# Masks of the second batch by matrix products, its maxima and differences from PSUM, one exponential per pair of heads

## Chip, cores and metric

One Trainium2 chip, one core of it. The metric is the device time in microseconds (us) of one launch; less is better. "PE" is TensorE, "DVE" VectorE, "ACT" ScalarE, "POOL" GpSimd, "SP" the queue that issues the DMAs.

## What is computed

Eight batches of windowed attention feed a two-layer feed-forward net. Cut to what matters:

```python
# q, k, v: (8, 8, 576, 64); heads 0..3 plain window of 32, heads 4..7 window 128, every 4th position
scores = 1/sqrt(64) * q @ k.T
scores = where(mask[head], scores, -1e9)
scores = scores - max(scores, axis=-1)
attn = exp(scores); attn = attn / (sum(attn, axis=-1) + 1e-9)
x = (attn @ v) as (4608, 512)
h = x @ w_in                       # (512, 2048)
out = where(h > 0, h, exp(min(h, 0)) - 1) @ w_out
```

## The kernel before

**Stages.** Attention of batch 0 runs first (`first_attention`, lines 338 to 386). Then the feed-forward net runs over the tokens: three passes of 512 tokens (`c` = 0, 1, 2), each with 16 steps `f` over the 2048 hidden columns, and after them a second form over larger blocks with fewer products. The attention of a later batch is woven into the pass before the tokens are needed; that of batch 1 (`second_attention`, lines 904 to 933) lies in pass `c` = 0, one or two pieces per step `f`.

**Batch 1.** It has four pairs of heads. A pair has two banks of scores in PSUM (`a_ps0`, `a_ps1`, one per head, 96 partitions by 6 x 64) and three pieces of work. E (lines 913 to 921): 72 small products for the scores, then on DVE masks added from PSUM into the SBUF tile `sm` (line 397), maxima over groups of 64 (line 410) and a scaling of the maxima (line 413), then on ACT six exponentials of 96x64, each with its own bias and with its sum accumulated (line 389). X (lines 422 to 436): six more such exponentials, the reciprocal of the sums on DVE (lines 326, 327), the product with them on POOL (line 328), 32x32 transposes on DVE (line 432), and copies into the operand `pt`, three on ACT and three on POOL (line 435). O (lines 924 to 932): products with `v` into the same two banks, then copies to `x32` on ACT (lines 314, 317). The pieces come in the order E0 X0 E1 X1 O0, a gap, E2 X2 O1, a gap, E3 X3, a gap, O2 O3. `sm` has a single buffer, so pair 1 may write it only when the copies of pair 0 have read it, and O0 may write the banks only when E1 has been read out of them.

**Beside it in pass 0.** The weights come as 64-bit floats. ACT scales the upper words (line 136), DVE puts 32-bit floats together in three steps (lines 144, 152, 154), and each is split into a high part on ACT and a low part on DVE (lines 191, 193). Step `f` computes a bank `h` (12 products of 512 columns, 8 with high weights and then 4 with low ones), ACT and DVE apply the activation (lines 627, 629, 632 or 634), and `o_ps` collects the second layer.

**Order.** PE works in program order: every product goes through `mm` (line 111). The other engines' order is made when the program is built, by a scheduler with an estimate of each instruction's duration, within `issue_after` bounds: the conversion of a weight block waits behind `maxima[-1]`, the splitting of x behind `masked[-1]`. So one changed piece moves neighbours on DVE, ACT and SP, up to the start of the second form, whose order is written out.

Of the kernel before, what the change touches and what calls it, by code (L numbers as in the profile page):

```python
# [15 lines left out]
AF = mybir.ActivationFunctionType  # L16
ALU = mybir.AluOpType
# [7 lines left out]
G = 32  # L25
QB = 3 * G
NU = S // QB
# [47 lines left out]
def body(ctx: ExitStack, tc: tile.TileContext, q, k, v, masks, w_in, w_out, out):  # L75
# [34 lines left out]
    def mm(*args, **kw):  # L110
        return inorder(nc.tensor.matmul(*args, **kw))  # L111
# [182 lines left out]
    def scores(s_ps, qt, kt, start):  # L294

        for n in range(NU):
            for c in range(GU):
                for h in range(2):
                    score(s_ps[h][:, n * 2 * G:(n + 1) * 2 * G], qt, kt, h, n, c, start, start or n == NU - 1)
# [85 lines left out]
        a_ps = ps_f.tile([P, 2, TC], F32, name="db"[hp % 2])  # L385
        yield outputs(0, hp, [(a_ps[:, i, :], i * NA, (i + 1) * NA) for i in range(NU // NA)], vt, tr, inorder)

    def exponential(u, sm, nmx, sums):
        nc.scalar.activation(out=sm[:, u, :], in_=sm[:, u, :], func=AF.Exp, bias=nmx[:, u:u + 1], scale=0.125, accum_out=sums[:, u:u + 1])  # L389

    def masks_added(hp, places, sm, eng=nc.vector):

        dil = hp >= NPAIR // 2
        for i in range(max(len(p) for p in places)):
            for h in range(2):
                n0, n1, s_ps = places[h][i]
                last = eng.tensor_tensor(out=sm[:, h * NU + n0:h * NU + n1, :].rearrange("p n j -> p (n j)"), in0=s_ps[:QB, :(n1 - n0) * 2 * G],  # L397
                                        in1=mask_sb[:, int(dil), n0 * 2 * G:n1 * 2 * G], op=ALU.add)
        return last

    def exponentials(b, hp, places, sm=None):

        if sm is None:
            sm = ap.tile([QB, 2 * NU, 2 * G], F32, name="sm", bufs=1)
            last = masks_added(hp, places, sm)
            if b == 1:
                masked.append(last.ins)
        nmx = ap.tile([QB, 2 * NU], F32, name="nmx", bufs=4)
        sums = ap.tile([QB, 2 * NU], F32, name="sums", bufs=4)
        nc.vector.tensor_reduce(out=nmx, in_=sm, op=ALU.max, axis=mybir.AxisListType.X)  # L410
        if b == 1:

            maxima.append(nc.vector.tensor_scalar(out=nmx, in0=nmx, scalar1=-0.125, scalar2=None, op0=ALU.mult).ins)
            for u in range(NU):
                exponential(u, sm, nmx, sums)
        else:
            nc.vector.tensor_tensor(out=sm, in0=sm, in1=nmx.unsqueeze(2).broadcast_to([QB, 2 * NU, 2 * G]), op=ALU.subtract)
            nc.scalar.activation(out=sm, in_=sm, func=AF.Exp, scale=0.125)
            nc.vector.tensor_reduce(out=sums, in_=sm, op=ALU.add, axis=mybir.AxisListType.X)
        return b, hp, sm, nmx, sums  # L420

    def probabilities(b, hp, sm, nmx, sums):

        if b == 1:

            for u in range(NU, 2 * NU):
                exponential(u, sm, nmx, sums)
        normalise(nc.gpsimd if b == 1 else nc.vector, sm, sums, lambda ins: ins)
        tr = transposed()
        for r in range(2):  # L430
            part = sm[:, :, r * G:(r + 1) * G]
            nc.vector.transpose(out=part, in_=part)  # L432
            for c in range(GU):
                ks, cs, rs = slice((c + r) * G, (c + r + 1) * G), slice(c * G, (c + 1) * G), slice(r * G, (r + 1) * G)
                last_transpose[b] = (nc.gpsimd.tensor_copy if r else nc.scalar.copy)(out=tr[ks, :, cs], in_=sm[cs, :, rs]).ins  # L435
        return b, hp, tr
# [467 lines left out]
    def second_attention():  # L904

        x32[1] = xp.tile([P, NPAIR, S], F32, name="x32", bufs=2)
        state = [None] * NPAIR

        for step in " E0 X0 E1 X1 O0  E2 X2 O1  E3 X3  O2 O3".split(" "):
            if step:  # L910
                what, hp = step[0], int(step[1])
                i = NPAIR + hp
                if what == "E":
                    s_ps = banks()
                    scores(s_ps, *qk_of.pop(i), True)
                    state[hp] = exponentials(1, hp, [[(0, NU, a)] for a in s_ps])
                    load_qk(i + 1)
                    if hp == 0:
                        load_v(i + 1)
                    if hp == NPAIR - 1:  # L920
                        load_qk(i + 2)
                elif what == "X":
                    state[hp] = probabilities(*state[hp])
                else:
                    b, _, tr = state[hp]
                    places = [(a, i * NA, (i + 1) * NA) for i, a in enumerate(banks())]
                    products(places, v_of.pop(NPAIR + hp), tr)
                    if hp < NPAIR - 1:
                        copies(b, hp, places)
                    else:  # L930
                        state[hp] = b, hp, places
                    load_v(i + 2)
            yield state[-1]
# [205 lines left out]
```

## Time and profile before

| | |
|---|---|
| runs | 871.54, 871.65, 874.05 us; median 871.65 |
| profiled execution | 872.5 us, span 870.7 us |
| mean granted TensorE clock | 0.996 |
| PE | busy 853.7 us of the span, 6788 products |
| DVE | busy 555.7 us, 902 instructions |
| ACT | busy 526.9 us, 1031 instructions |
| POOL | busy 75.0 us, 112 instructions |
| longest chain | 84% of the span on PE |

The time is the launch as the device counts it; the span is the part with instructions in the profile, 1.8 us less in this execution. Busy shares are means over all stages. What a change in one stage is worth has to be read in that stage: which engine is full there, and who waits for whom.

### The profile page before, as it was taken

The numbers are of one execution on the slowest core, as the hardware profiler recorded it, in microseconds if no ns is written. First come the engines' busy times: TensorE is split into PE (matmuls) and PEld (weight loads), VectorE is DVE, ScalarE is ACT, GpSimd is POOL, SyncE is SP. The second block draws the span as 40 slices with busy tenths as digits, with TensorE's granted clock in tenths as the row PEclk, the third lists the DMA queues.
The fourth block names the chain that finished last, engine by engine and source line by source line (L and its number), as shares of the span: only waits on it lengthen the run. The fifth ranks groups of instructions, "written<-read, shape, count | busy, mean of one in ns | idle before, by whom it ended". The sixth has DMA issues, their size and how long they took to land.

```text
span 870.7 us, 17559 instructions
## 1 busy us (share of the span) xinstructions
PE 853.7 (98%) x6788; PEld 722.5 (83%) x6788; DVE 555.7 (64%) x902; ACT 526.9 (61%) x1031; POOL 75.0 (9%) x112
## 2 busy tenths in 40 slices
PE   6999999999999999999999999999999999999998
PEld 4556878888878889888878898988899988999986
DVE  6899987766685857787765577545476635344431
ACT  3767987756585756667654575654566654555541
POOL 2013311000020200111010020100011100000000
PEclk8999999999999999999999999999999999999999
DMA  9997335134546346867753867662875652776441
GB/s 343 378 381 264 132 123 188 34 132 133 176 160 200 102 151 215 262 221 239 231 173 100 279 200 242 212 184 83 265 226 175 206 164 80 241 209 191 143 153 56
DMA packets 93459, 166.48 MB, mean 191 GB/s; under 512 B 9696, under 2 KB 40768, under 8 KB 93376
## 3 DMA queue, kind: packets, MB, share of 16 engines
q1 hardware_dynamic: 89200, 158.01, 57.0%
q10 hardware_dynamic: 4176, 7.34, 2.3%
q8 instruction: 54, 0.88, 0.4%
q14 instruction: 29, 0.24, 0.1%
HBM read 124.42 MB, written 40.89 MB: 190 GB/s over the span
## 4 chain that ended last, share of the span: by engine, by line
PE 84%; DVE 7%; ACT 4%; DMA 2%; issue 2%; POOL 1%; SPq 0%; ACTq 0%; DVEq 0%; POOLq 0%
PE o_ps L111 41%; PE h L111 34%; PE a_ps L111 8%; DVE a L152 1%; DMA out<-e 1%; POOL pt L435 1%; DVE a L154 1%; DMA r<-combined 1%; DVE nmx L410 1%; ACT sm L389 0%; ACT pt L383 0%; DVE sm L397 0%; PE a L111 0%; DMA kt<-k 0%; DVE a L144 0%
## 5 line engine op out<-in xcount | busy, mean ns | idle before, releaser
L111 PE MATMUL h<-xall,r 128*128 128x384 f32 (+1 forms) x708 | 156.9, 363 | 0.4 <-DVE e L634 0.2
L111 PEld LDWEIGHTS h<-xall,r 128*128 128x128 f32 x708 | 127.7, 188 | 17.2 <-issue 0.8
L111 PE MATMUL o_ps<-a,gh 128*128 128x512 f32 x394 | 129.0, 416 | 0.0
L448 DVE SCALAR_TENSOR_TENSOR a-1_3369<-a-1_3369,a 128x768 f32<-128x768 f32 x64 | 61.0, 953 | 87.9 <-ACT a L448 87.9
L111 PE MATMUL h<-r,r 128*128 128x384 f32 x476 | 108.3, 337 | 0.4 <-DMA r<-combined 0.4
L448 ACT COPY e<-h 128x384 f32<-128x384 f32 x96 | 46.0, 479 | 98.5 <-PE h L111 96.6
L111 PEld LDWEIGHTS o_ps<-a,gh 128*128 128x128 f32 x394 | 73.4, 188 | 21.8 <-issue 9.1
L448 ACT ACTIVATE a<-a-1_3369 128x384 f32<-128x384 f32 (+1 forms) x96 | 60.8, 634 | 50.0 <-DVE a-1_3369 L448 44.0
L111 PEld LDWEIGHTS h<-r,r 128*128 128x128 f32 x476 | 84.4, 188 | 4.0 <-ACT e L448 0.7
L111 PE MATMUL o_ps<-r,gh 128*128 128x512 f32 x242 | 75.4, 393 | 0.0
L111 PE MATMUL o_ps<-a,r 128*128 128x512 f32 x288 | 72.3, 392 | 0.0
L111 PE MATMUL o_ps<-a,gl 128*128 128x512 f32 x173 | 67.7, 391 | 0.0
L448 ACT ACTIVATE a<-a 128x768 f32<-128x768 f32 (+1 forms) x72 | 60.8, 845 | 1.9
L111 PEld LDWEIGHTS o_ps<-a,r 128*128 128x128 f32 x288 | 53.7, 188 | 9.9
L111 PE MATMUL h<-a,r 128*128 128x384 f32 x256 | 60.1, 336 | 0.0
L448 DVE TENSOR_TENSOR a-1_3369<-h,e 128x384 f32<-128x384 f32 x64 | 35.2, 550 | 34.8 <-PE h L111 34.7
L111 PEld LDWEIGHTS o_ps<-r,gh 128*128 128x128 f32 x242 | 44.9, 188 | 8.6
L111 PEld LDWEIGHTS h<-a,r 128*128 128x128 f32 x256 | 46.4, 188 | 4.2
L111 PE MATMUL o_ps<-r,gl 128*128 128x512 f32 x117 | 46.0, 393 | 0.2 <-DVE gl L448 0.2
L435 POOL COPY pt<-sm 32x384 f32<-32x384 f32 x36 | 32.9, 913 | 103.1 <-DVE sm L432 102.1
L111 PE MATMUL o_ps<-a,xall 128*128 128x512 f32 x153 | 39.5, 393 | 0.0
L637 DVE SCALAR_TENSOR_TENSOR e<-h,e 128x512 f32<-128x512 f32 x30 | 20.9, 696 | 27.1 <-ACT e L636 27.1
(219 smaller groups left out, 1553.6 us busy)
## 6 DMA issues: line engine op xcount, KB each, us to landing
r<-combined SPq DMA_DIRECT2D x224, 256.0 KB, 3.6
aside<-a-1_3369 SPq DMA_DIRECT2D x64, 192.0 KB, 3.4
vt<-v SPq DMA_DIRECT2D x30, 384.0 KB, 4.4
kt<-k SPq DMA_DIRECT2D x30, 304.0 KB, 4.9
qt<-q SPq DMA_DIRECT2D x30, 288.0 KB, 4.2
r<-w_in SPq DMA_DIRECT2D x16, 512.0 KB, 7.9
r<-w_out SPq DMA_DIRECT2D x16, 512.0 KB, 8.3
combined<-a SPq DMA_DIRECT2D x20, 256.0 KB, 3.2
```

Of the source, the lines that this page charges most:

```text
L111: return inorder(nc.tensor.matmul(*args, **kw))
L152: keep(nc.vector.scalar_tensor_tensor(out=au, in0=hi, scalar=0x80000000, in1=au, op0=ALU.bitwise_and, op1=ALU.bitwise_or))
L154: return keep(nc.vector.scalar_tensor_tensor(out=au, in0=lo, scalar=29, in1=au, op0=ALU.logical_shift_right, op1=ALU.bitwise_or))
L410: nc.vector.tensor_reduce(out=nmx, in_=sm, op=ALU.max, axis=mybir.AxisListType.X)
L435: last_transpose[b] = (nc.gpsimd.tensor_copy if r else nc.scalar.copy)(out=tr[ks, :, cs], in_=sm[cs, :, rs]).ins
L448: return lambda *args, **kw: inorder(getattr(self.eng, name)(*args, **kw))
L637: v.scalar_tensor_tensor(out=e, in0=h_ps, scalar=0.0, in1=e, op0=ALU.max, op1=ALU.subtract)
```

## The change

In E of batch 1, both banks first get the masks by a product of the unit matrix `ones_sb` with `mask_sb` (96x384, bf16), and the scores are accumulated on top, as batch 0 already does. DVE takes the maxima from each bank, subtracts them from the bank and writes the difference to `sm`. One exponential of 96x768 on ACT follows, and one sum over groups on DVE. The six exponentials in X are gone. The scheduling bounds `masked` and `maxima` now both point at the last difference.

```diff
-    def exponential(u, sm, nmx, sums):
-        nc.scalar.activation(out=sm[:, u, :], in_=sm[:, u, :], func=AF.Exp, bias=nmx[:, u:u + 1], scale=0.125, accum_out=sums[:, u:u + 1])
...
-            last = masks_added(hp, places, sm)
-            if b == 1:
-                masked.append(last.ins)
+            if b > 1:
+                masks_added(hp, places, sm)
...
-        nc.vector.tensor_reduce(out=nmx, in_=sm, op=ALU.max, axis=mybir.AxisListType.X)
+        wide = lambda x, n: x.unsqueeze(2).broadcast_to([QB, n, 2 * G])
         if b == 1:
-
-            maxima.append(nc.vector.tensor_scalar(out=nmx, in0=nmx, scalar1=-0.125, scalar2=None, op0=ALU.mult).ins)
-            for u in range(NU):
-                exponential(u, sm, nmx, sums)
+            heads = [(slice(h * NU, (h + 1) * NU), a[:QB, :NU * 2 * G].rearrange("p (n j) -> p n j", n=NU)) for h, a in enumerate(places)]
+            for part, s3 in heads:
+                nc.vector.tensor_reduce(out=nmx[:, part], in_=s3, op=ALU.max, axis=mybir.AxisListType.X)
+                last = nc.vector.tensor_tensor(out=sm[:, part, :], in0=s3, in1=wide(nmx[:, part], NU), op=ALU.subtract)
+            masked.append(last.ins)
+            maxima.append(last.ins)
         else:
...
+        nc.scalar.activation(out=sm, in_=sm, func=AF.Exp, scale=0.125)
+        nc.vector.tensor_reduce(out=sums, in_=sm, op=ALU.add, axis=mybir.AxisListType.X)
         return b, hp, sm, nmx, sums
...
-        if b == 1:
-
-            for u in range(NU, 2 * NU):
-                exponential(u, sm, nmx, sums)
...
                     s_ps = banks()
-                    scores(s_ps, *qk_of.pop(i), True)
-                    state[hp] = exponentials(1, hp, [[(0, NU, a)] for a in s_ps])
+                    for a in s_ps:
+                        mm(a[:QB, :NU * 2 * G], ones_sb, mask_sb[:, int(hp >= NPAIR // 2), :], start=True, stop=False)
+                    scores(s_ps, *qk_of.pop(i), False)
+                    state[hp] = exponentials(1, hp, s_ps)
```

In the changed kernel unchanged code after this point stands 3 to 5 lines higher: the activation on DVE is line 627 there (632 before), the transposes 427 (432), the copies to `pt` 430 (435), the copy of `h` 619 (624), the stores' copies 673 (678).

First place, PE at E0, the only kind of difference that PE has (it comes four times); the differences between the two programs:

```order
 L111 MATMUL h_567<-x_142,a_357 128x512 x4
+L111 LDWEIGHTS masks_sb
+L111 MATMUL a_ps_581<-masks_sb 96x384
+L111 LDWEIGHTS masks_sb
+L111 MATMUL a_ps_582<-masks_sb 96x384
 L111 MATMUL a_ps_581<-kt,qt 32x64
 L111 MATMUL a_ps_582<-kt,qt 32x64
```

Two products of 384 columns come ahead of the 72 of the scores, and nothing else on PE moves.

Second place, DVE from the conversion beside E0 and E1 to the activation ahead of O0; here the change is in more than the added instructions. Before:

```order
L193 TENSOR_TENSOR h<-a_538,h 128x512
L413 TENSOR_SCALAR nmx<-nmx 96x12
L154 SCALAR_TENSOR_TENSOR a_538<-r_281,a_538 128x1024
L144 TENSOR_SCALAR a_638<-a_638 128x2048
L152 SCALAR_TENSOR_TENSOR a_638<-r_523,a_638 128x2048
L193 TENSOR_TENSOR gl<-a_538,gl 128x512
L326 TENSOR_SCALAR sums<-sums 96x12
L154 SCALAR_TENSOR_TENSOR a_638<-r_523,a_638 128x2048
L327 RECIPROCAL sums<-sums 96x12
L632 SCALAR_TENSOR_TENSOR gh<-h_688,e 128x512
L144 TENSOR_SCALAR a_769<-a_769 128x2048
L193 TENSOR_TENSOR h<-a_638,h 128x512
```

and now, from the sum of pair 0 on:

```order
L418 TENSOR_REDUCE sums<-sm 96x12
L154 SCALAR_TENSOR_TENSOR a_538<-r_281,a_538 128x1024
L144 TENSOR_SCALAR a_636<-a_636 128x2048
L326 TENSOR_SCALAR sums<-sums 96x12
L627 SCALAR_TENSOR_TENSOR gh<-h_680,e 128x512
L152 SCALAR_TENSOR_TENSOR a_636<-r_523,a_636 128x2048
L327 RECIPROCAL sums<-sums 96x12
L410 TENSOR_REDUCE nmx<-a_ps_702 96x6
L410 TENSOR_REDUCE nmx<-a_ps_703 96x6
L193 TENSOR_TENSOR gl<-a_538,gl 128x512
L154 SCALAR_TENSOR_TENSOR a_636<-r_523,a_636 128x2048
L144 TENSOR_SCALAR a_759<-a_759 128x2048
```

Ahead of the low part `gl` for step `f` = 4 there now stand the sum (line 418), the activation (627), the reciprocal (327) and the two maxima of E1 (410). Behind the last row come the two transposes (427), then both L193 of the next steps, then the activation, then the two differences of E1; before, the two L193 stood ahead of the transposes.

Third place, ACT around the start of pass `c` = 2, where no instruction of batch 1 lies, but the schedule shifts. Before:

```order
L624 COPY h<-h_2661 128x512
L418 ACTIVATE sm<-sm 96x768
L627 ACTIVATE e<-h 128x512
L678 COPY e<-o_ps_1723 128x512
L678 COPY e<-o_ps_1727 128x512
L636 ACTIVATE e<-e 128x512
L678 COPY e<-o_ps_1731 128x512
L678 COPY e<-o_ps_1735 128x512
L642 CAST gh<-e 128x512
L247 CAST e<-a_2255 128x512
L435 COPY pt_79<-sm 32x12x32 x3
L624 COPY h<-h_2723 128x512
```

and now:

```order
L417 ACTIVATE sm<-sm 96x768
L619 COPY h<-h_2629 128x512
L622 ACTIVATE e<-h 128x512
L673 COPY e<-o_ps_1691 128x512
L673 COPY e<-o_ps_1695 128x512
L631 ACTIVATE e<-e 128x512
L673 COPY e<-o_ps_1699 128x512
L430 COPY pt_79<-sm 32x12x32 x3
L637 CAST gh<-e 128x512
L673 COPY e<-o_ps_1703 128x512
L247 CAST e<-a_2223 128x512 x2
L619 COPY h<-h_2691 128x512
```

The copy that empties the bank `h` (line 624, now 619) has moved behind the exponential of the woven attention, and the next one behind both L247.

## Rows read from the trace of the kernel before

**Rows 1.** The page, busy time of each engine, its share of the span and its instructions.

```profile
PE 853.7 (98%) x6788; PEld 722.5 (83%) x6788; DVE 555.7 (64%) x902; ACT 526.9 (61%) x1031; POOL 75.0 (9%) x112
```

**Rows 2.** What PE waited for over the whole span: us in total, times, longest. Of these rows the first lies at the start of passes 1 and 2 (1.2 us of it at 246 us), the others in pass 0.

```profile
PE h L111 <- ACT h L624: 1.4, 2, 1.2
...
PE h L111 <- DVE h L193: 1.0, 1, 1.0
...
PE a_ps L111 <- PE h L111: 0.3, 1, 0.3
...
PE h L111 <- DVE e L634: 0.2, 1, 0.2
```

**Rows 3.** Busy time by stretch, in the stretch of E0, X0 and E1: us, then each engine with its instructions, granted clock, DMA share, GB/s.

```profile
50.00:60.00 10.00, 10.00 (x31) 5.64 (x30) 10.00 (x11) 7.94 (x22) 1.47 (x1) 1.00 0.99 357
```

**Rows 4.** DVE by line and shape: mask additions and maxima of batch 1 (30 to 120 us), and the difference from PSUM in batch 0 (0 to 30 us); busy us, mean ns of one, idle before.

```profile
L397 DVE TENSOR_TENSOR sm<-a_ps,masks_sb 96x384 f32<-96x384 f32 x8 | 4.0, 545 | 2.1 <-POOL pt L435 2.1
L410 DVE TENSOR_REDUCE nmx<-sm 96x12 f32<-96x768 f32 x4 | 3.8, 940 | 0.0
...
L359 DVE TENSOR_TENSOR sm<-a,nmx 96x768 f32<-96x768 f32 x1 | 1.0, 953 | 0.0
```

**Rows 5.** ACT by line and shape, 0 to 135 us: the small exponentials of batch 1 and one large one of batch 0.

```profile
L389 ACT ACTIVATE sm<-sm,nmx 96x64 f32<-96x64 f32 x48 | 16.0, 338 | 9.3 <-DVE nmx L413 9.3
...
L361 ACT ACTIVATE sm<-sm 96x768 f32<-96x768 f32 x1 | 0.8, 844 | 6.8 <-DVE sm L359 6.8
```

**Rows 6.** PE's timeline in batch 0: one pair of mask products and the 72 score products behind it (start us, us).

```profile
9.15 0.87 PE L111 MATMUL a<-masks_sb 96*96 96x384 bf16 x2
9.96 1.52 PE L111 MATMUL a<-r 64*32 64x64 f32 x72
```

**Rows 7.** PE's timeline in pass 0 (start us, us): the low products of step 3, scores of E1, steps 4 and 5, O0, O3.

```profile
47.63 1.19 PE L111 MATMUL h<-xall,h 128*128 128x512 f32 x4 [1.03 <-DVE h L193]
48.75 0.97 PE L111 MATMUL a_ps<-kt,qt 64*32 64x64 f32 x72
...
52.78 3.32 PE L111 MATMUL h<-xall,gl 128*128 128x512 f32 x12
...
58.97 3.30 PE L111 MATMUL h<-xall,h 128*128 128x512 f32 x12
62.56 1.23 PE L111 MATMUL a_ps<-pt,vt 128*64 128x96 f32 x24 [0.29 <-PE h L111]
...
126.17 1.21 PE L111 MATMUL a_ps<-pt,vt 128*64 128x96 f32 x24
```

**Rows 8.** DVE's timeline, the instructions that the sum uses (start us, us).

```profile
48.71 1.21 DVE L144 TENSOR_SCALAR a<-a 128x2048 uint32<-128x2048 uint32 x1
...
52.16 0.68 DVE L193 TENSOR_TENSOR gl<-a,gl 128x512 fp32r<-128x512 f32 x1
...
52.84 2.28 DVE L154 SCALAR_TENSOR_TENSOR a<-r,a 128x2048 uint32<-128x2048 uint32 x1
55.04 0.22 DVE L327 RECIPROCAL sums<-sums 96x12 f32<-96x12 f32 x1
...
55.72 2.26 DVE L144 TENSOR_SCALAR a<-a 128x2048 uint32<-128x2048 uint32 x1
...
59.11 1.02 DVE L432 STREAM_TRANSPOSE sm<-sm 96x384 f32<-96x384 f32 x2
60.06 0.65 DVE L632 SCALAR_TENSOR_TENSOR gh<-h,e 128x512 f32<-128x512 f32 x1
61.91 1.02 DVE L397 TENSOR_TENSOR sm<-a_ps,masks_sb 96x384 f32<-96x384 f32 x2 [1.20 <-POOL pt L435]
...
75.78 2.96 DVE L154 SCALAR_TENSOR_TENSOR a<-r,a 128x2048 uint32<-128x2048 uint32 x1
...
80.19 0.67 DVE L634 SCALAR_TENSOR_TENSOR e<-h,e 128x512 f32<-128x512 f32 x1
```

**Rows 9.** POOL's timeline: products with the reciprocals and copies to `pt`, the row of 79.85 being the first of its three copies alone.

```profile
55.43 1.47 POOL L328 TENSOR_TENSOR sm<-sm,sums 96x768 f32<-96x768 f32 x1 [35.05 <-DVE sums L327]
60.29 1.58 POOL L435 COPY pt<-sm 32x384 f32<-32x384 f32 x3 [3.39 <-DVE sm L432]
74.90 1.70 POOL L328 TENSOR_TENSOR sm<-sm,sums 96x768 f32<-96x768 f32 x1 [13.03 <-DVE sums L327]
79.85 3.71 POOL L435 COPY pt<-sm 32x384 f32<-32x384 f32 x1 [3.26 <-DVE sm L432]
...
122.96 1.87 POOL L435 COPY pt<-sm 32x384 f32<-32x384 f32 x3 [2.19 <-DVE sm L432]
```

**Rows 10.** The start of pass 2: ACT's timeline, then PE's (start us, us).

```profile
236.83 0.59 ACT L624 COPY h<-h 128x512 f32<-128x512 f32 x1 [3.73 <-PE h L111]
238.40 0.85 ACT L418 ACTIVATE sm<-sm 96x768 f32<-96x768 f32 x1 [0.99 <-DVE sm L417]
...
243.94 1.55 ACT L435 COPY pt<-sm 32x384 f32<-32x384 f32 x3
245.52 0.58 ACT L624 COPY h<-h 128x512 f32<-128x512 f32 x1
...
239.35 2.88 PE L111 MATMUL h<-xall,r 128*128 128x512 f32 x12
...
246.16 3.03 PE L111 MATMUL h<-xall,a 128*128 128x512 f32 x12 [1.21 <-ACT h L624]
```

More of the change, by code (lines that the diff above doesn't have):

```diff
@@ L404, in exponentials @@
             sm = ap.tile([QB, 2 * NU, 2 * G], F32, name="sm", bufs=1)
-            last = masks_added(hp, places, sm)
-            if b == 1:
-                masked.append(last.ins)
+            if b > 1:
+                masks_added(hp, places, sm)
         nmx = ap.tile([QB, 2 * NU], F32, name="nmx", bufs=4)
         sums = ap.tile([QB, 2 * NU], F32, name="sums", bufs=4)
-        nc.vector.tensor_reduce(out=nmx, in_=sm, op=ALU.max, axis=mybir.AxisListType.X)
+        wide = lambda x, n: x.unsqueeze(2).broadcast_to([QB, n, 2 * G])
         if b == 1:
-            maxima.append(nc.vector.tensor_scalar(out=nmx, in0=nmx, scalar1=-0.125, scalar2=None, op0=ALU.mult).ins)
-            for u in range(NU):
-                exponential(u, sm, nmx, sums)
-        else:
-            nc.vector.tensor_tensor(out=sm, in0=sm, in1=nmx.unsqueeze(2).broadcast_to([QB, 2 * NU, 2 * G]), op=ALU.subtract)
-            nc.scalar.activation(out=sm, in_=sm, func=AF.Exp, scale=0.125)
-            nc.vector.tensor_reduce(out=sums, in_=sm, op=ALU.add, axis=mybir.AxisListType.X)
+            heads = [(slice(h * NU, (h + 1) * NU), a[:QB, :NU * 2 * G].rearrange("p (n j) -> p n j", n=NU)) for h, a in enumerate(places)]
[4 more added lines that the diff above has]
+            maxima.append(last.ins)
+        else:
+            nc.vector.tensor_reduce(out=nmx, in_=sm, op=ALU.max, axis=mybir.AxisListType.X)
+            nc.vector.tensor_tensor(out=sm, in0=sm, in1=wide(nmx, 2 * NU), op=ALU.subtract)
+        nc.scalar.activation(out=sm, in_=sm, func=AF.Exp, scale=0.125)
+        nc.vector.tensor_reduce(out=sums, in_=sm, op=ALU.add, axis=mybir.AxisListType.X)
         return b, hp, sm, nmx, sums
     def probabilities(b, hp, sm, nmx, sums):
-        if b == 1:
-            for u in range(NU, 2 * NU):
-                exponential(u, sm, nmx, sums)
         normalise(nc.gpsimd if b == 1 else nc.vector, sm, sums, lambda ins: ins)
```

## The prediction

> **What bounds the kernel now.** I read the busy times first: PE is busy for 98% of the span, DVE and ACT for under two thirds [rows 1]. So a saving on ACT or DVE counts only where PE waits for it. The list of PE's waits is the second view, and it is short [rows 2]: 1.0 us for a low weight part from DVE, 0.3 at O0, 0.2 for an activation, and 1.4 for ACT at the starts of later passes, 2.9 us in all. That is the most that relief of the other engines can give back. The third view, busy time by stretch, shows the danger: while E0, X0 and E1 run, DVE is busy 10.00 of 10 us [rows 3]. There, whatever is put on DVE delays what stands behind it. The timelines [rows 7 to 9] tell how far PE is from noticing.
>
> **What the change removes and adds.** *ACT*, per pair: twelve exponentials of 0.338 us each go, one of 0.844 comes [rows 5], some 3.2 us less on an engine that PE does not wait for in that stage; worth nothing by itself. *DVE*, per pair: two mask additions (0.545 each) and one maximum over both heads (0.940) go, with the small scaling. Two maxima and two differences from the bank come, each half of a 96x768 instruction: 0.940 and 0.953 whole [rows 4], and a mask addition of that half size from PSUM takes 0.545, so I take 0.54 each, between 0.47 and 0.55. One sum (0.94, as the maximum) comes too. That is about 1 us more per pair, which must be seen in place. *PE*, per pair: two products of 384 columns. In batch 0 a pair takes 0.81 us, from 9.15 to the scores at 9.96, but PE was slower there: the same 72 scores take 1.52 us against 0.97 in pass 0 [rows 6, 7]. Scaled by that, 0.52. From the other side, 12 products of 512 columns take 2.7 us with the weights ready, from the 2.88 of a step less the overlap at its end [rows 10], or 0.17 for 384 columns: 0.34 a pair. I take 0.45, nearer to the row that is scaled for speed than to the raw one, and keep 0.34 and 0.81.
>
> **Step 3, beside E0.** PE waits here for the low part on DVE and resumes at 47.63 [rows 7]. Ahead of it DVE had two additions and a maximum and now has two maxima and two differences: four times 0.47 start to start against 1.79 us, so +0.07 us. E0's mask products disappear in the wait of 1.03. PE is 0.07 late at E1's products (48.75), 0.5 late with their masks at step 4 (53.3 for 52.78).
>
> **Step 4.** The low part for it started on DVE at 52.16 [rows 8], far ahead of need. In the new order the sum (0.94), the activation (0.65), the reciprocal (0.22) and E1's two maxima (1.0) stand in front of it. Instructions overlap by about 0.08 at their ends (52.84 and 2.28 against a start at 55.04), so it comes some 2.5 us later, at 54.7. POOL now meets it: the product of pair 0 starts 0.39 after the reciprocal starts (55.04 and 55.43) and takes 1.47 [rows 8, 9], thus from 54.0 to 55.5. What happens when the two meet, the trace shows twice: the DVE instruction at 55.72 took 2.26, where the same took 1.21 at 48.71, and the one at 75.78 took 2.96, where 2.28 is usual; both ended as if they had started when POOL's instruction was over (56.90, 76.60) [rows 8, 9]. So the low part runs from 55.5 to 56.2. PE wants it after 8 of the step's 12 products, at 53.3 plus two thirds of 3.3, or 55.45: a wait of 0.8.
>
> **O0.** DVE goes on from 56.2 with a 2.28 instruction, then one of 1.21 that no longer meets POOL, then the transposes (1.02) [rows 8], to 60.5. POOL's copies to `pt` could start. But two low parts (0.68 each) now stand right behind the transposes, to 61.7, and a copy beside a row of such instructions took 3.71 us, against 0.53 for each of the three at 60.29, which ran beside the activation at 60.06 [rows 8, 9]. I let the copies wait for the low parts, but not for the activation behind them, as the nearest row (60.29) has it: 61.7 to 63.3. `sm` has one buffer, so the first difference of E1 comes then, 0.54, and O0 starts at 63.9, where it was 62.56 [rows 7]: PE is 1.35 late, of which it waits 0.45 here (step 5, from 58.97, would be done at 63.45). Bounds: with no meeting of DVE and POOL there is no wait at step 4, the copies end at 61.4 and PE is limited by its own products, 0.1 late; with POOL let in only when DVE stands still (62.3), O0 starts at 64.5, 1.95 late. The Trainium skill (SBUF — State Buffer, section on who interferes with whom) says that a VectorE instruction with two SBUF inputs and a GpSimd one that reads SBUF exclude each other for the whole instruction, while one with at most one SBUF input does not disturb GpSimd. By that the copies get in during the activation, and the sum is 2.85; the trace has a row against it, the copy from 79.85, which stayed out although the activation at 80.19 reads one SBUF operand; by that row the sum would be 3.45 [rows 8, 9]. My value goes by the row at 60.29 either way.
>
> **E2, O1, E3.** The maxima moved ahead of the differences give POOL room, and PE is by then later than DVE by more than the added instructions. I cost the neighbours at nothing here: their cover is PE's own lateness of 1.35. If it were gone, the low parts would be late next. The masks of E2 and E3 cost 0.9 (0.68 to 1.62). The 0.2 for an activation in step 14 goes, since PE comes later.
>
> **Start of pass 2.** No instruction of batch 1 is here, but ACT's order changed. The copy that empties `h` ran at 236.83, now it stands behind the exponential (238.40 and 0.85), so it ends at 239.85 and PE, ready at 239.35, waits 0.5. The next such copy at 245.52, for which PE already waited 1.21 [rows 10], has the first copy (0.59) and one more cast (0.5) between it and the exponential: 1.1 later, less idle time of ACT before it. I take 0.8, within bounds of 0 (the idle time covers all) and 1.1. Two low-part casts move here too; PE is not near them. SP's queue changes by pairs of neighbours, whose DMAs no row shows PE waiting for; nothing.
>
> **Sum.** 1.35 + 0.9 - 0.2 + 0.8 = 2.85 us later. On the profiled execution, 872.5, that is 875.35; this execution stands 0.85 over the median of 871.65, so the forecast is 874.5. Bounds: 0.1 + 0.68 - 0.2 + 0 = 0.6, or 872.2, and 1.95 + 1.62 + 1.1 = 4.7, or 876.3.
>
> **Rivals.** *Hidden* (not slower): POOL and DVE do not hold each other in the new order, and ACT's idle time covers pass 2. For it: POOL's product may start a little earlier or later than the low part, by half a us. Against: two rows that show the hold. Only three mask pairs are paid, +0.6 to +0.9: 872.4. It decides if the low part for step 4 ends before 55.45. *O3 waits* (slower still): the copies of pair 3 ended at 124.83 and O3 began at 126.17 [rows 7, 9], 1.3 to spare. The reciprocal of that pair now stands behind two activation instructions (1.3 us) and a sum. PE is 2.05 later itself, so I think it holds; if the copies end after 128.2, each us is PE's. Price 1.5: 876.0. *Relief* (faster): ACT's shorter queue and the new order take away all 2.9 us of waits [rows 2], and four mask pairs cost 0.34 each: -1.5, or 870.1; with masks partly in gaps 868.8. For it: ACT really loses 3.2 us per pair. Against: none of the waits in pass 0 ends with an exponential of batch 1.
>
> **Numbers.** Forecast 0.45, hidden 0.34, O3 waits 0.13, relief 0.08. About 0.3%, or 2.6 us, is what a measurement of this kernel can tell from no change, and the forecast of +2.85 lies right at it: I count 0.27 of its 0.45 as slower and 0.18 as same. With 0.13 of O3, slower is 0.40. Hidden and half of relief add to same: 0.56. Faster keeps 0.04. The range goes from 871.0, which leaves out most of relief, to 877.0, which takes in O3 and the upper bound.
>
> **What would show it.** Right: eight more products and PE's wait at step 4 near 0.8 for DVE, with the low part of that step longer than 1 us or starting at POOL's end; O0's start near 64; waits for the copy of `h` near 240 and 247 us (both later by the shift so far). The mask pair shows its price between its start and the scores. Wrong: no wait in step 4, or a low part of 0.68 beside POOL's product; then hidden holds. A wait of O2 or O3 for `pt`: the second rival. Waits in pass 0 that are shorter than now in sum: relief. If PE's sum of waits grows at places not named here, for instance in pass 1, the error is in what I cost at nothing.

## Result and profile after

The changed kernel takes 877.56 us (median of 5 runs, 876.09 to 879.0) where the kernel before, on the same chip, took 873.38 (5 runs, 871.54 to 874.05): ratio 1.0052, 95% interval 1.0033 to 1.0072. It is slower by some 4.5 us, above the forecast of 874.5 and above the upper end of its range, 877.0. A second measurement gave 1.0053 (1.0038 to 1.0068). The forecast set out from 871.65, the median of three runs of the kernel before; with the two more taken beside the changed kernel it is 873.38. So 1.7 of the 3.1 us by which 874.5 was missed lie in the starting value, and 1.3 in the loss (4.2 between the medians, 2.85 forecast). One later execution, of 945 us at a granted clock of 0.85, is left out of all times and of the table.

The profiled execution took 879.0 us, span 877.2, mean granted clock 0.996 as before. PE's busy time grew by 2.4 us for eight more products [rows 1], so most of the loss is waiting:

```profile
PE 856.1 (98%) x6796; PEld 722.4 (82%) x6796; DVE 557.1 (64%) x906; ACT 514.9 (59%) x939; POOL 80.5 (9%) x112
```

The list of PE's waits after (engine, tile and line, what it waited for: us in all, times, longest); the first lines, batch 0's, are left out:

```profile
PE h L111 <- ACT h L619: 1.9, 3, 1.0
PE o_ps L111 <- DVE gl L638: 1.3, 1, 1.3
PE h L111 <- DVE h L193: 1.1, 1, 1.1
PE h L111 <- issue: 0.9, 2, 0.5
...
PE h L111 <- DVE gl L193: 0.6, 1, 0.6
```

Against [rows 2] two waits in pass 0 are new: 0.6 for the low part of step 4, which was forecast, and 1.3 for `gl` of line 638, which was not. The copy of `h` (line 619) costs 1.9 where it cost 1.4. The 0.9 under "issue", for which the profile names no cause, lies at 285 and 631 us.

**Where the time went.** I laid each profile beside the first one of the kernel before: for every PE product, its start minus the start of the same product (in program order) before. The table has the growth of this shift by stretch, in us; each column adds up to the shift at the end. "Sums on ACT" and the others are the experiments below.

| stretch (us, before) | forecast | after | after, again | before, again (two) | masks alone | sums on ACT | conversion behind `gl` | product on DVE | loads behind stores |
|---|---|---|---|---|---|---|---|---|---|
| batch 0 (to 30) | 0 | 0.64 | 1.00 | -0.28, 0.09 | 0.04 | 1.57 | 0.72 | 0.58 | 1.13 |
| E0, E1 (to 53) | 0.50 | 0.42 | 0.40 | 0.01, -0.01 | 0.35 | 0.38 | 0.42 | 0.39 | 0.39 |
| step 4 (to 58) | 0.8 | 0.91 | 0.89 | -0.01, 0.01 | 0.01 | 0.01 | 0.89 | 0.01 | 0.91 |
| O0 (to 70) | 0.05 | -0.33 | -0.34 | 0, -0.02 | -0.36 | -0.36 | -0.32 | 4.75 | -0.32 |
| E2, E3 (to 110) | 0.9 | 0.62 | 0.63 | -0.01, 0 | 0.62 | 0.63 | 0.62 | 0.63 | 0.61 |
| steps 11 to 15 (to 140) | -0.2 | 1.06 | 1.02 | -0.13, -0.19 | -0.48 | -0.57 | 0.92 | -0.58 | 0.99 |
| start of pass 1 (to 155) | 0 | 1.07 | 1.12 | -0.29, 0.71 | 1.13 | 0.05 | 1.34 | 0.57 | -0.20 |
| start of pass 2 (235 to 260) | 0.8 | 0.46 | 0.46 | 0.02, 0.02 | 0.02 | 0.01 | 0.43 | 0 | 0.43 |
| the rest | 0 | 1.62 | 1.33 | -0.64, 0.07 | -0.56 | 0.16 | 0.84 | -0.97 | 0.24 |
| end | 2.85 | 6.47 | 6.51 | -1.33, 0.68 | 0.77 | 1.88 | 5.86 | 5.38 | 4.18 |

Two things are to be seen. From 30 to 110 us the executions of one kernel agree within 0.05 us in each stretch, and from 110 to 140 us within 0.2, so tenths can be read there; in "the rest" no more than a us or two can. And both profiled executions of the changed kernel took 879.0 us, the upper end of its runs, so they overstate the loss.

**Step 4.** DVE of the changed kernel (start, duration, line, operation, x count, idle time before it and what ended it), then POOL:

```profile
52.03 2.27 DVE L152 SCALAR_TENSOR_TENSOR a<-r,a 128x2048 uint32<-128x2048 uint32 x1
54.23 0.21 DVE L327 RECIPROCAL sums<-sums 96x12 f32<-96x12 f32 x1
54.36 0.94 DVE L410 TENSOR_REDUCE nmx<-a_ps 96x6 f32<-96x384 f32 x2
55.23 1.57 DVE L193 TENSOR_TENSOR gl<-a,gl 128x512 fp32r<-128x512 f32 x1
56.73 2.28 DVE L154 SCALAR_TENSOR_TENSOR a<-r,a 128x2048 uint32<-128x2048 uint32 x1
...
61.59 0.98 DVE L193 TENSOR_TENSOR gl<-a,gl 128x512 fp32r<-128x512 f32 x1
62.50 0.68 DVE L627 SCALAR_TENSOR_TENSOR gh<-h,e 128x512 f32<-128x512 f32 x1
63.52 1.02 DVE L411 TENSOR_TENSOR sm<-a_ps,nmx 96x384 f32<-96x384 f32 x2 [0.35 <-POOL pt L430]
```

```profile
54.61 1.64 POOL L328 TENSOR_TENSOR sm<-sm,sums 96x768 f32<-96x768 f32 x1 [33.50 <-DVE sums L327]
61.24 2.24 POOL L430 COPY pt<-sm 32x384 f32<-32x384 f32 x3 [4.99 <-DVE sm L427]
```

The low part of step 4 takes 1.57 us instead of the 0.68 of [rows 8], and ends 0.55 after POOL's product; PE waits 0.60 for it. Later the copies to `pt` end at 63.48 and E1's first difference starts at 63.52: the queue at O0 that the prediction describes, with one difference: the copies did not wait for the low parts. The first one ran beside them and was over at 62.03, and the second low part took 0.98 us for it. O0's products start at 64.19, where 63.9 was forecast.

**Step 11 and pair 3.** DVE again:

```profile
111.25 1.00 DVE L411 TENSOR_TENSOR sm<-a_ps,nmx 96x384 f32<-96x384 f32 x2
112.18 1.20 DVE L193 TENSOR_TENSOR r<-a,r 128x1024 fp32r<-128x1024 f32 x1
113.31 2.28 DVE L152 SCALAR_TENSOR_TENSOR a<-r,a 128x2048 uint32<-128x2048 uint32 x1
115.52 1.21 DVE L193 TENSOR_TENSOR r<-a,r 128x1024 fp32r<-128x1024 f32 x1
116.65 0.68 DVE L638 TENSOR_TENSOR gl<-e,gh 128x512 fp32r<-128x512 f32 x1
117.25 0.94 DVE L418 TENSOR_REDUCE sums<-sm 96x12 f32<-96x768 f32 x1
...
122.19 0.21 DVE L327 RECIPROCAL sums<-sums 96x12 f32<-96x12 f32 x1
...
125.44 1.03 DVE L427 STREAM_TRANSPOSE sm<-sm 96x384 f32<-96x384 f32 x2 [1.37 <-POOL sm L328]
129.96 1.23 DVE L443 TENSOR_TENSOR r<-a,r 128x1024 fp32r<-128x1024 f32 x1 [3.48 <-ACT r L443]
```

```profile
115.50 0.61 PE L111 MATMUL o_ps<-r,gh 128*128 128x512 f32 x2
117.38 0.50 PE L111 MATMUL o_ps<-r,gl 128*128 128x512 f32 x1 [1.26 <-DVE gl L638]
```

In the changed kernel the conversion's first long step (line 152, 2.28 us) stands ahead of `gl`. Before, its bound `maxima[-1]` pointed at the scaling, which stood behind `gl` (113.38 and 112.78 in that profile), and kept it there; now the bound points at the differences (111.25) and lets it go first. It does not force that order: with the sums on ACT, below, the bound is the same and `gl` stands first. So `gl` comes at 117.33. Second, the sum of pair 3, whose exponential is over at 113.20, gets its turn at 117.25, and the reciprocal at 122.19 (118.64 before). The transposes, ACT's copies to `pt` and the first weights of pass 1 behind them on ACT all come 3.7 us later (125.44 and 129.96 for 121.78 and 126.28).

**Start of pass 1.** The chain that ended last, in order of time:

```profile
145.08 0.48 ACT e L673
145.56 0.03 issue
145.59 4.93 DMA out<-e
...
150.62 0.58 ACT e L673
...
152.67 0.50 ACT h L619
```

ACT's fourth copy of pass 0's output needs the buffer of the first; the first store took 4.93 us to land (3.87 before), and the copy of `h` for which PE then waits 1.0 stands behind that copy.

### The profile page after: what moved, and what is told of

It is laid out like the page before. It is cut to its first block, busy times and chain, and to the rows that moved or that the text cites. A ratio compares the mean times of both kernels' runs of the same rounds, so it can differ in the third digit from the quotient of the medians.

```text
span 877.2 us, 17484 instructions
## 1 busy us (share of the span) xinstructions
PE 856.1 (98%) x6796; PEld 722.4 (82%) x6796; DVE 557.1 (64%) x906; ACT 514.9 (59%) x939; POOL 80.5 (9%) x112
## 4 chain that ended last, share of the span: by engine, by line
PE 86%; DVE 4%; ACT 4%; DMA 3%; issue 1%; SPq 0%; POOL 0%; ACTq 0%; DVEq 0%
PE o_ps L111 42%; PE h L111 35%; PE a_ps L111 8%; DMA r<-combined 1%; DVE a L152 1%; DMA whole<-a 1%; DMA out<-e 1%; DMA kt<-k 1%; ACT a L136 0%; ACT pt L383 0%; PE a L111 0%; DMA vt<-v 0%; PE b L111 0%; ACT e L673 0%; DVE r L193 0%
## 5 line engine op out<-in xcount | busy, mean ns | idle before, releaser
L430 POOL COPY pt<-sm 32x384 f32<-32x384 f32 x36 | 36.6, 1016 | 102.5 <-DVE sm L427 101.5
L637 ACT CAST gh<-e 128x512 fp32r<-128x512 f32 x38 | 23.6, 621 | 29.0 <-DVE e L632 16.6
```

The costliest lines, as they stand in the source:

```text
L637: high.append(a.copy(out=gh, in_=e).ins)
```

## Experiments

Theory A: the loss comes from the order on DVE, that is from where the sum and the conversion stand. B: it is scatter. C: the products on PE are the cost. D: DVE and what hangs on it is too full there, so a wait that is taken away comes back further on.

### The kernel before, twice more

> The kernel before, profiled once more, to learn how far two executions of one program drift apart, place by place. Theory A (order of instructions): the changed kernel lost its time at named places: 1.0 us net up to O0, 0.33 at each of E2 and E3, 1.5 at the low part gl of step 11, 1.1 at the start of pass 1, 0.4 at the start of pass 2, 0.8 at 279 us; so here every one of these places should show a shift under 0.3 us against the first profile, and the span should agree within 1 us apart from the first 30 us. Theory B (scatter): the later places (start of pass 1, start of pass 2, 279 us) belong to the scatter of stores landing; then shifts of 0.5 to 1 us appear here too at the starts of passes.

> The kernel before, on this chip, for the places where batch 0 starts and where scatter is at issue. If the first kt lands at 5.0 to 5.6 us as in the two other profiles of it and in two kernels with half of the change, and at 5.9 to 6.6 in the changed kernel's, the difference belongs to the program and not to the chip or the day; if it lands at 5.9 or later here, it is scatter. Shifts up to 400 us within 0.3 us of the first profile's.

871.15 and 873.18 us. Up to 110 us their shifts change by under 0.03 us from stretch to stretch after batch 0, from there to 140 us by -0.13 and -0.19; the start of pass 1 moves by -0.29 and +0.71, beyond the 0.3 that was expected. So B is out for pass 0, and not for the start of pass 1 nor for "the rest". The first `kt` landed in time for scores at 5.15 and 5.46 us, as in the first profile, which by the second expectation speaks for the program and against the chip or the day.

### The changed kernel again

> The changed kernel once more. Theory A (the loss is made by the order of instructions): the shifts of PE against the kernel before come back at the same places and sizes within 0.3 us: E0 and E1 +0.3 to 0.4 each (E0 taken back), step 4 +0.9, E2 and E3 +0.33 each, step 11 at 113.7 us +1.5 with a wait for the low part near 1.3 us, the start of pass 1 +1.1 with a wait for the copy of h near 1.0. Theory B (scatter): the place at 148 us, whose wait ends with the landing of a store, changes by over 0.5 us, as do the shifts at 283.9, 347 and 625 us. Time 876 to 879 us by either.

878.97 us, ratio 1.0053 (1.0038 to 1.0068). Every stretch from 30 to 155 us came back within 0.06 us, and the start of pass 2 too. A holds in pass 0; the places at 279 and 625 us of the kernel before changed by 0.4 and 0.7, as B says. But scatter is not all of it: the three profiles of the kernel before agree at these two places within 0.01 us, and the changed kernel lost 0.78 and 0.40 at the first, 0.59 and 1.29 at the second.

### One half each: the masks alone, the exponential alone

The masks alone, against the kernel before (the products on PE as in the change, not shown; maxima, scaling and twelve exponentials as before):

```diff
-            last = masks_added(hp, places, sm)
+            for h, a in enumerate(places):
+                last = nc.vector.tensor_copy(out=sm[:, h * NU:(h + 1) * NU, :].rearrange("p n j -> p (n j)"), in_=a[:QB, :NU * 2 * G])
```

The exponential alone (masks added on DVE as before; the six exponentials in X go too, not shown):

```diff
-            maxima.append(nc.vector.tensor_scalar(out=nmx, in0=nmx, scalar1=-0.125, scalar2=None, op0=ALU.mult).ins)
-            for u in range(NU):
-                exponential(u, sm, nmx, sums)
+        last = nc.vector.tensor_tensor(out=sm, in0=sm, in1=nmx.unsqueeze(2).broadcast_to([QB, 2 * NU, 2 * G]), op=ALU.subtract)
+            maxima.append(last.ins)
+        nc.scalar.activation(out=sm, in_=sm, func=AF.Exp, scale=0.125)
+        nc.vector.tensor_reduce(out=sums, in_=sm, op=ALU.add, axis=mybir.AxisListType.X)
```

> Of the change only the mask products on PE; DVE then copies the banks to sm (same size as the additions of before), maxima, scaling and twelve small exponentials stay as before. Theory A: PE pays 0.42 us for three of the four pairs (E0's lies in a wait), 1.3 us in pass 0, no wait at step 4 and none for gl of step 11; +1.0 to +1.6 us (872.9 to 875), as DVE's order stays. Theory C (the products themselves are the cost, also through what they push back): most of the loss of the change, +3 us or more, shows here already.

> Of the change only the single exponential: masks are still added on DVE, then maxima, difference, one exponential, sum as in the later batches; no mask products. DVE does two additions (0.95), maximum, difference and sum (0.86 each start to start), some 1.75 us more per pair than before, 0.9 more than in the changed kernel. Theory A: PE has no product more, but the waits at step 4 and O0 are at least as long as in the changed kernel (0.6 and more), +1 to +3 us. Theory C: without the products on PE nothing is lost, within 0.5 us of before.

Masks alone: 874.17 us, ratio 1.0017 (1.0004 to 1.003). The products cost 0.31 to 0.33 each at E1, E2 and E3, and PE's coming later takes back 0.36 at O0 and 0.50 at 116 us, where PE had waited for an activation: 0.14 in all of pass 0. C falls. What it lost, 1.13, lies at the start of pass 1. So A's time (872.9 to 875) came true by luck: it had 1.3 us in pass 0 and nothing behind it.

The exponential alone: 883.42 us, ratio 1.0122 (1.0096 to 1.0148), the worst of all and 10 us over the kernel before, where A had 1 to 3. At step 4 it loses nothing (-0.02), against A; at O0 4.93, in steps 11 to 15 2.75, at the start of pass 1 1.75. Its list of PE's waits:

```profile
PE a_ps L111 <- DVE sm L397: 3.7, 1, 3.7
...
PE h L111 <- ACT h L616: 2.6, 4, 1.1
...
PE a_ps L111 <- POOL pt L427: 1.7, 1, 1.7
```

O0 waits 3.7 us until E1's masks are in `sm`, O3 waits 1.7 for pair 3's copies, the second rival of the prediction. The sum belongs to both this kernel and the change. What comes late here are the instructions that read the banks: E1's masks start at 64.79, behind an activation for which DVE had waited 2.44 us, where the change has its differences at 63.52.

### Conversion behind the low part of step 11

```diff
-    last_conversion = convert(ready // 2, behind=maxima[-1] if maxima else None)
+    last_conversion = convert(ready // 2, behind=low[-1] if ready == 14 else maxima[-1] if maxima else None)
```

> The changed kernel with one bound of its schedule altered: the last two conversion steps of the last weight block wait behind the low part gl of the step before, where they waited behind the difference of the last pair. Theory A: the wait of 1.26 us at the products of step 11 goes, PE is 1.0 to 1.5 us earlier from there on than in the changed kernel, all else in pass 0 the same; the total falls by about that (876) if the later passes keep their waits. Theory D (DVE is simply too full: the delay only moves): the wait turns up again within pass 0, for a weight part of steps 13 to 15 or O3, and PE is not earlier at the end of pass 0.

> The changed kernel with the conversion of step 14 held behind the low part of step 11, again, for a profile that can be laid beside the others. Theory A: the wait of 1.26 us of o_ps at 117.38 is gone (under 0.4 us left), and if nothing moves, the time is 1.2 us less, near 876.3. Theory D (DVE is too full there, so the delay only moves on): the wait is gone but another of 0.8 to 1.3 us stands behind it in steps 12 to 15 or at the starts of the next pieces, and the time stays within 0.5 us of the changed kernel's.

878.59 us, ratio 1.0059 (1.0042 to 1.0076), and 878.47, 1.0059 (1.0043 to 1.0075). In the second, on DVE:

```profile
112.23 2.34 DVE L193 TENSOR_TENSOR r<-a,r 128x1024 fp32r<-128x1024 f32 x2
114.50 0.67 DVE L638 TENSOR_TENSOR gl<-e,gh 128x512 fp32r<-128x512 f32 x1
115.10 2.27 DVE L152 SCALAR_TENSOR_TENSOR a<-r,a 128x2048 uint32<-128x2048 uint32 x1
117.30 0.93 DVE L418 TENSOR_REDUCE sums<-sm 96x12 f32<-96x768 f32 x1
...
122.24 0.21 DVE L327 RECIPROCAL sums<-sums 96x12 f32<-96x12 f32 x1
...
130.00 1.22 DVE L443 TENSOR_TENSOR r<-a,r 128x1024 fp32r<-128x1024 f32 x1 [3.48 <-ACT r L443]
```

and what PE and its weight loads wait for between 126 and 140 us:

```profile
PEld h L111 <- DVE xall L443: 0.7, 2, 0.4
PEld o_ps L111 <- DVE r L443: 0.5, 1, 0.5
```

`gl` comes 2.15 us sooner and the wait of 1.26 is gone. But the sum, the reciprocal and the first weights of pass 1 stand where they stood (117.30, 122.24, 130.00 for 117.25, 122.19, 129.96), and PE waits for these in place of `gl`. First it waits 0.43 us, at 118.89, for the activation that stands behind the sum (118.17); then, by now only 0.77 earlier than in the change, it has two gaps of 0.38 at 131 and 133 us (as the kernel before counts). The stretch from 110 to 140 gives 0.92 instead of 1.06. D holds here, with three small waits for the one that it had: the chain of pair 3 sets when pass 0 ends, and the wait at step 11 only says where PE does its waiting.

### POOL's two parts

```diff
 copies on ACT:
-    (nc.gpsimd.tensor_copy if r else nc.scalar.copy)(out=tr[ks, :, cs], in_=sm[cs, :, rs])
+    (nc.gpsimd.tensor_copy if r and b > 1 else nc.scalar.copy)(out=tr[ks, :, cs], in_=sm[cs, :, rs])
 product on DVE:
-    normalise(nc.gpsimd if b == 1 else nc.vector, sm, sums, lambda ins: ins)
+    normalise(nc.vector, sm, sums, lambda ins: ins)
```

> The changed kernel with the three copies to pt that POOL makes per pair of batch 1 made by ACT. Theory A: O0's idle time of 0.35 us for pt on DVE goes and the 9.64 us that the three copies took at 99.39 too, but PE's waits at step 4 (0.6) and step 11 (1.26) stay, as they hang on POOL's product and the conversion: 877 to 878 us. Rival (POOL's copies slow the DVE instructions that they run beside): DVE's instructions between 99 and 111 us get shorter together, step 11's low part comes at least 0.8 us sooner, its wait falls under 0.5 us: 876 to 876.7 us.

> The changed kernel with batch 1's products with the reciprocals on DVE instead of POOL: no instruction of POOL over SBUF pairs is left beside DVE's in these steps. Theory A (POOL's product holds the DVE instruction that meets it until its end): the low part of step 4 takes 0.68 us instead of 1.57 and ends about 0.6 us sooner (the product, about 0.95 us, now stands ahead of it on DVE), so that PE's wait of 0.6 goes to 0 to 0.2; the transposes at 98 us don't wait 1.37, and step 11's low part comes 0.8 to 1.4 us sooner, its wait 0 to 0.5: 875.3 to 876.5 us. Rival D (DVE is full, 0.95 us more per pair on it delays as much as the hold did): the waits at steps 4 and 11 stay at 0.5 or more and 1.2 or more, 877 to 879.5 us.

Copies on ACT: 878.26 us, ratio 1.0046 (1.003 to 1.0063). The wait at step 4 stays (0.6), that at step 11 is 0.8, and O3 now waits 0.7 for ACT's copies, with 0.93 more at 131 and 133 us: 2.25 from 110 to 140. Neither theory had that wait, and the 0.8 lies between the 1.26 of A and the rival's 0.5.

Product on DVE: 878.45 us, ratio 1.0054 (1.0039 to 1.0069). The low part of step 4, without POOL beside it:

```profile
55.15 0.69 DVE L193 TENSOR_TENSOR gl<-a,gl 128x512 fp32r<-128x512 f32 x1
```

It starts within 0.08 us of the 55.23 above and takes 0.69 instead of 1.57, and PE's wait at step 4 is gone: POOL's product was what held it. The rest of A's forecast failed. The product now stands at 59.08 on DVE and the transposes come at 61.76, 1.7 us later than in the change. On ACT, the copies to `pt` stand ahead of the next activation:

```profile
62.37 1.55 ACT L430 COPY pt<-sm 32x384 f32<-32x384 f32 x3 [2.63 <-DVE sm L427]
63.95 0.60 ACT L622 ACTIVATE e<-h 128x512 f32<-128x512 f32 x1
64.58 0.63 ACT L624 ACTIVATE e<-e 128x512 f32<-128x512 f32 x1
```

ACT waits 2.63 us for the transposes, DVE then 2.44 for the activation (65.24), and E1's differences stand behind that: O0 waits 3.4 us. (In the kernel with the exponential alone the same waits read 2.69, and 2.44 on DVE.) The wait costs more than itself: behind it the granted clock is 0.83 from 66 to 68 us and 0.50, the lower of its two levels (1.2 and 2.4 GHz), from 68 to 70 (1.00 in the change), and the products of O0 and the step after it add some 1.6 us to the 3.1 by which O0 starts later. From there PE is so late that steps 11 to 15 cost it nothing. The same time came out by another way.

### The sums back on ACT

For batch 1 alone, with only the lines that matter:

```diff
 mask products, maxima and differences from the bank as in the change, then
-    nc.scalar.activation(out=sm, in_=sm, func=AF.Exp, scale=0.125)
-    nc.vector.tensor_reduce(out=sums, in_=sm, op=ALU.add, axis=mybir.AxisListType.X)
+    # six in E, six in X, without bias
+    nc.scalar.activation(out=sm[:, u, :], in_=sm[:, u, :], func=AF.Exp, scale=0.125, accum_out=sums[:, u:u + 1])
```

> The changed kernel with the mask products and the maxima and differences from the bank, but the exponentials again twelve per pair on ACT, which make the sums as they go; DVE's sum (0.94 us a pair) is gone. Theory A (the sum and its place on DVE, behind the conversion's 2.3 us instruction, is what makes pair 3's reciprocal come at 122.2 us, 9 us after its exponential, and step 4's low part late): the low part of step 4 comes 0.9 us sooner and no product of POOL holds it, so PE's wait there of 0.6 is gone; the reciprocal of pair 3 comes at 118 to 120 us; PE's shift at 140 us, less that at 30, is 0.5 to 1.6 us instead of 2.5 to 2.7, and the time 1 to 2 us less than the changed kernel's, 875.5 to 877 us. The loss of 0.46 at the start of pass 2 goes too. Rival (the differences, which hold sm until pt is copied, or the products on PE are the loss): the shift at 140 us stays at 2.3 or more and the time within 0.5 us of the changed kernel's.

873.29 us, ratio 1.0006 (0.9997 to 1.0016). DVE:

```profile
53.72 0.69 DVE L193 TENSOR_TENSOR gl<-a,gl 128x512 fp32r<-128x512 f32 x1
54.32 0.22 DVE L327 RECIPROCAL sums<-sums 96x12 f32<-96x12 f32 x1
...
111.82 0.68 DVE L648 TENSOR_TENSOR gl<-e,gh 128x512 fp32r<-128x512 f32 x1
112.43 2.28 DVE L152 SCALAR_TENSOR_TENSOR a<-r,a 128x2048 uint32<-128x2048 uint32 x1
...
117.50 0.21 DVE L327 RECIPROCAL sums<-sums 96x12 f32<-96x12 f32 x1
```

Step 4's low part comes 1.5 us sooner and ahead of POOL's product; `gl` of step 11 stands ahead of the conversion; pair 3's reciprocal comes 4.7 us sooner, though its exponentials take ACT from 110.34 to 113.80 us instead of 0.85 us. The waits that the change added in pass 0 are gone; the 1.0 at step 3 is left, as before. From 30 to 140 us PE loses 0.09 us where the change loses 2.68. The loss at the start of pass 2 is gone too. A predicted 0.5 to 1.6 here, the reciprocal at 118 to 120 and 875.5 to 877; the gain was larger, 4.1 us by the ratios (1.0053 less 1.0006, of 873). By the table 2.6 of it lie in pass 0, 0.45 at the start of pass 2, and 1.0 at the start of pass 1, where executions of one kernel differ by as much. The run changes the sum and the number of exponentials together, and no run parts them; in pass 0 it is DVE's order that differs, at the start of pass 2 ACT's.

### The loads at the start of pass 1

```diff
-    load_qk(b * NPAIR + hp + 2, b > CS)
+    load_qk(b * NPAIR + hp + 2, b > CS or (b, hps[0]) == (2, 0))
...
+    if (c, f) == (1, 2):
+        with tc.issue_after(stores[-1]):      # the last store of pass 0's output
+            load_next(4)
```

> The changed kernel with one thing moved: the four loads of qt and kt that SP issues at the start of pass 1, 4.35 us ahead of the first store of pass 0's output, are issued right behind the four stores; every other engine's order is as in the changed kernel. Theory S (at the start of pass 1 the first store lands late, at 4.93 us after its issue, because the loads' data are in its way; before they were issued 4.69 us ahead and the store took 3.87): the first store lands within 3.5 us, ACT's fourth copy has no idle time for it (1.5 now), PE's shift between 140 and 155 us is between -0.3 and +0.3 instead of +1.07 to +1.13, and the time is 1.1 to 1.4 us less than the changed kernel's, 876.3 to 877.5. Rival (the loads are not it: ACT itself, or the stores' own weight): the store still takes over 4.4 us, the shift stays at 0.8 or more, the time within 0.5 us of the changed kernel's.

> The kernel with the mask products alone (maxima over a copy, twelve exponentials, as before), with the same four loads behind the stores. The kernel without that move lost 0.1 us in pass 0 and 1.13 at the start of pass 1. Theory S: the second loss goes, the ratio to the kernel before is 0.999 to 1.001. Rival: it stays, 1.001 to 1.003.

With the change: 876.86 us, ratio 1.0052 (1.0037 to 1.0067). ACT's third and fourth copies now follow each other without idle time,

```profile
148.99 1.05 ACT L675 COPY e<-o_ps 128x512 f32<-128x512 f32 x2
```

and the stretch gives -0.20 instead of +1.07: the first store, issued at 145.97, had landed within 3.5 us. The loads were in the first store's way. The time does not show it: 1.0052 and 1.0053 cannot be told apart. With the masks alone: 872.44 us, ratio 0.9999 (0.999 to 1.0009), the stretch -0.14 for +1.13; the ratio without the move was 1.0017, and the two intervals just overlap.

With the loads in their old place the stretch follows the first store's time, from its issue to the start of the fourth copy. In the nine executions where that copy waited for it: 3.96 us (first profile of before) gives 0, 4.02 0.05, 4.44 0.49, 4.53 0.57, 4.68 (before, third) 0.71, 5.03 and 5.10 (the changed kernel) 1.07 and 1.12, 5.10 (masks alone) 1.13, 5.32 1.34. How much of the change's 1.1 is its own and how much chance is open, since one of three executions of the kernel before lost 0.71. Some of it seems to be its own: where the first of the four loads was issued 4.69 to 4.74 us ahead of the store (the kernel before three times, product on DVE, sums on ACT) that time was 4.68 at most (3.68 where the copy had no wait for it), and where it was issued 4.20 to 4.35 ahead (the change twice, masks alone, conversion, copies) 4.44 to 5.32.

## Why the prediction was wrong

**Held, by size.** E0's mask products vanished in PE's wait (0.33 more, 0.28 back). Step 4: the low part came behind the sum, met POOL's product and was held; a wait of 0.8 forecast, 0.60 measured. O0: late by 1.35 forecast, by 1.0 measured (0.42 + 0.91 - 0.33), since the whole old wait at O0 was taken back and the forecast kept 0.45. The time of O0 came out nearly right although the copies to `pt` started beside the low parts, where the forecast had them wait. The mask pairs: 0.45 each forecast, 0.31 net measured, below the bound of 0.34 that I had for the products themselves, since part of them lies in an issue gap ahead of the scores. The copy of `h` at the start of pass 2 behind the one exponential: PE 0.57 later for 0.5 forecast, and gone with the sums on ACT. The other half of that term was wrong: the second copy was to cost more, but PE's wait for it fell from 1.21 to 0.56, while PE lost 0.50 in between, waiting for a copy of the output. In sum 0.46 for 0.8:

```profile
242.75 0.85 ACT L417 ACTIVATE sm<-sm 96x768 f32<-96x768 f32 x1 [5.30 <-DVE sm L416]
243.51 0.56 ACT L619 COPY h<-h 128x512 f32<-128x512 f32 x1
```

```profile
244.12 3.03 PE L111 MATMUL h<-xall,r 128*128 128x512 f32 x12 [0.30 <-ACT h L619]
...
250.94 3.04 PE L111 MATMUL h<-xall,a 128*128 128x512 f32 x12 [0.56 <-ACT h L619]
```

**The step that failed** is this one: "I cost the neighbours at nothing here: their cover is PE's own lateness of 1.35." Two neighbours used up that cover and more. The bound of the conversion moved ahead of `gl` of step 11: `gl` came 3.9 us later while PE was 2.3 late, which cost 1.5 us, of which 0.5 came back 2.7 us later. And the sum of pair 3 came behind the conversion's first long step, a low weight part and `gl`; with its own time and two more instructions ahead of the reciprocal, that put the reciprocal 3.5 us later. In the change itself PE meets that second chain without a wait, having waited before; with the first wait taken away it cost as much. Instead of -0.2, steps 11 to 15 cost 1.06 and 1.02. The prediction did name the low parts as what would be late next, and the late reciprocal of pair 3 under O3; it didn't work out when. The tightness could be read before: `gl` ran from 112.78 to 113.45 and PE used it at 113.70, 0.25 to spare. Pass 0 came to 2.68 and 2.60 for the forecast 2.05.

**Costed at nothing too,** and not mechanisms of the forecast: the start of pass 1 (1.07 and 1.12, the store that waits behind the loads), and batch 0 (0.64 and 1.00). Without these 1.7 us, which the profiled executions may overstate, the median would lie inside the range. It would also lie inside if the range were moved up by the 1.7 us of the starting value: the loss of 4.5 us is within the sum's bounds of 0.6 to 4.7.

**The rivals.** Hidden fell with the hold at step 4. O3 did not wait in the change, but did in two experiments (1.7 and 0.7), as that rival described. Relief fell, and the reason given against it stands: PE never waits for batch 1's exponentials. What I had wrong behind it is the value of that work on ACT ("worth nothing by itself"): the twelve exponentials kept a sum off DVE.

**What is open.** The scores of batch 0 wait for the first `kt`, issued at 1.65 us in every profile. They began at 5.15 to 5.55 us in six executions (three of the kernel before, two with the masks alone, one with the exponential alone), and at 5.88 to 6.64 in all eight of kernels that take the differences from the bank. SP issues the same DMAs at the same times up to 4 us, the sums on ACT had the latest start (6.64) and still the time of the kernel before, and no run tells what makes it.

## What to carry to other kernels

Price an instruction that is moved from an idle engine to a full one by the chain behind it, not by its own duration: here 0.94 us of sum per pair on DVE, with one exponential for twelve, cost 4.1 us. When a scheduler orders the engine, follow each result from its last producer to PE in the new order, and compare its slack with how late PE will be; here a slack of 0.25 us in the old profile was gone at once. And take away a wait only after looking at what else hangs on the same engine: here it came back within 20 us in nearly the same size.

## What the runs showed that was not expected

- POOL's three copies to `pt`, 1.58 us together beside one activation of DVE [rows 9], took 9.64 us from 99.39 in the changed kernel, the first alone 5.61, beside a row of DVE instructions most of which have two SBUF inputs. The change made only part of it: the same three copies took 6.17 from 98.15 in the kernel before. The Trainium skill (SBUF — State Buffer, section on who interferes with whom) says that such DVE instructions and a GpSimd one that reads SBUF exclude each other for the whole instruction; the trace agrees, at step 4 in the other direction (1.57 us beside POOL's product, 0.69 without). As the prediction words the other half of that rule, without the page's exception for the two-port modes, the one-input instruction at 55.72 [rows 8], which was held, would contradict it. The first of the three copies ended at 105.00, just behind the first activation in that row (104.27 to 104.95), which reads one SBUF operand; in the kernel before it ended at 102.86, beside the activation from 102.43.
- The pair of mask products, which took 0.81 us in batch 0 [rows 6], adds 0.31 to 0.33 to PE's program in pass 0.
- At the same place of the program a store of 256 KB took between 4.0 and 5.3 us, counted to the copy that needs its buffer, in nine executions, and PE's lateness there followed it one to one.
